# Two attentions share visits to TensorE: riders in one h buffer, turns without beats, and a third engine for the row scaling

## The chip, the cores and the metric

The kernel runs on one core of a Trainium2 chip. The core has TensorE (PE in the profile: matmuls; PEld: its weight loads), VectorE (DVE), ScalarE (ACT), GpSimd (POOL) and a queue of SyncE (SP) that issues the transfers. The metric is the time of one execution on the chip in microseconds, as the median of several runs.

## The reference

A cross attention compresses each batch of 12608 rows to 32 rows h, a second attention lets every row attend to h, and every resulting row goes through a gated layer with a softmax, a normalization and a second weight matrix.

```python
B, N, m, C = (4, 12608, 32, 128)
n_tokens, d_model, d_ff = (50432, 128, 1024)

def mab(q, kv):
    s = scale * (q @ kv.transpose(0, 2, 1))
    s = s - s.max(-1, keepdims=True)
    a = np.exp(s)
    a /= a.sum(-1, keepdims=True) + 1e-09
    return a @ kv
h = mab(I, x)
return mab(x, h).astype(np.float32)
...
h = x @ w_in
h_max = np.max(h, axis=-1, keepdims=True)
e = np.exp(h - h_max)
sm = e / (np.sum(e, axis=-1, keepdims=True) + 1e-09)
solu = h * sm
mu = np.mean(solu, axis=-1, keepdims=True)
var = np.mean((solu - mu) ** 2, axis=-1, keepdims=True)
ln = (solu - mu) / np.sqrt(var + 1e-06) * g_ln
return (ln @ w_out).astype(np.float32)
```

All of it is float32 for the matmuls.

## The kernel before

The rows of a batch are cut into 99 tiles of 128 (the last one shorter), 396 tiles in all. Line numbers here are those of the kernel before.

**The tile's path** (`main` and `soft`). Since h has 32 rows, the second attention's output times `w_in` is the attention's weights times a 32 x 1024 matrix `hs`, made once a batch in `combine`. So a tile's first product is 8 matmuls of 32 rows (line 946) into an h buffer, 128 x 1024 numbers in PSUM. VectorE scales it and takes its minimum (line 984), which frees h. ScalarE takes the exps with their sum (line 994), GpSimd multiplies (line 998), ScalarE squares and sums (line 1009), and VectorE turns blocks of 32 x 32 into `vt` (line 1022). When the four tiles of a group are turned, two streams `products` of 32 steps each follow on TensorE (line 1067), one on row groups 0 and 1 of the array, one on 2 and 3. Their results are evacuated by VectorE or ScalarE (line 1089), and `finish` scales the rows by the normalization, on ScalarE as four instructions (line 1144) or on GpSimd as one (line 1140).

**The attentions.** `p1(b, k)` is the first attention of twelve tiles of batch b: turns of x (line 550), scores (line 654), a small matmul for the common maximum (line 679), exps (line 705), sums (line 736). Batch 0 does this ahead of everything (the `early` branches); for later batches it lies among the tiles of the batch before. `p2(b, j)` is the second attention of up to twelve tiles: scores (line 844), their turning and maximum on VectorE (lines 851 and 853), exps, turns of the weights (line 550), copies (line 885).

**The two h buffers.** Outside the early part, PSUM has two h buffers and two buffers for the streams. A tile's first product, each turn, each score block and each block of sums takes an h buffer and gives it back when its last reader is done. For the scores of `p1` the last reader are the exps.

**Beats.** The first products and the turns use two of TensorE's four row groups. `beats` puts single steps of the stream that uses the other two between them. `turned_rows` turns three blocks to a beat. What uses all rows of the array (scores, sums, the small matmuls) is a visit of its own; the planner charges `SWITCH` = 400 ns for it.

**The order.** A planner (class `Planner`) writes the order of each engine ahead of time: it plays the program through with a cost for each operation, a latency for each crossing between engines (`AFTER`), and priorities (`PR_...`, in tiles). An operation with an alternative (`alt`) goes to the engine that can start it first. Each engine then runs its instructions in that order and waits on semaphores. So a change of a cost or of a priority moves instructions on all engines.

```python
pick = min(
    (o for o in self.ops if o[0].eng == eng and o[1] <= limit),
    key=lambda o: (o[2][1] if o[0].prio is None else o[0].prio, o[3]),
)
```

Of the kernel before, what the change touches and what calls it, by code (L numbers as in the profile page):

```python
# [14 lines left out]
ALU = mybir.AluOpType  # L15
# [5 lines left out]
C = 128  # L21
M = 32
FF = 1024
# [3 lines left out]
PG = 12  # L27
AG = 12
JB = FF // M
JC = 1  # L30
BEAT = 225
EAGER = 120
SWITCH = 400


def cut(total, most, unit):
# [17 lines left out]
TURNS = 3  # L54
HN_MORE = 4
# [3 lines left out]
LATE = -15  # L59
P1_FROM = 5  # L60
P1_GO = -10
P1_STEP = 7.5
P2_AHEAD = 35
P2_START = 24
PR_EX = 1
PR_EV = -20
PR_FI = 20
PR_G2 = 2
PR_HN = -2
PR_MU = 2  # L70
# [3 lines left out]
SLACK = {"PE": 0, "ACT": 100, "DVE": 300, "POOL": 0, "SP": 0}  # L74
# [5 lines left out]
AFTER = {  # L80
    "PE": {"PE": 0, "ACT": 237, "DVE": 236, "POOL": 240, "SP": 290},
    "ACT": {"PE": 245, "ACT": 143, "DVE": 182, "POOL": 101, "SP": 90},
    "DVE": {"PE": 296, "ACT": 168, "DVE": 127, "POOL": 195, "SP": 90},
    "POOL": {"PE": 245, "ACT": 115, "DVE": 114, "POOL": 100, "SP": 90},
    "SP": {"PE": 1076, "ACT": 1040, "DVE": 960, "POOL": 1040, "SP": 1000},
}
# [39 lines left out]
class Planner:  # L126
# [26 lines left out]
    def _step(self, task, value):  # L153
        gen = task[0]
        while True:
# [4 lines left out]
            if isinstance(want, Op):  # L160
                self.seq += 1
                for op in (want, want.alt):
                    if op is None:
                        continue
# [5 lines left out]
                    self.ops.append((op, start, task, self.seq))  # L170
                return
# [75 lines left out]
def set_attention_then_solu_kernel(ctx: ExitStack, tc: tile.TileContext, x, inducing, w_in, w_out, g_ln, out):  # L247
# [66 lines left out]
    EW = Lock()  # L314
# [261 lines left out]
    turned = [Event() for _ in range(NP)]  # L576

    def p1(b, k):
# [35 lines left out]
        for w in () if early else range(2):  # L614
            tr, trel = yield ltr
            d = yield turned_rows(tr, [(xn[:, s, :], P) for s in range(n)], w, RUSH, [d for d, _ in xd], trel)
            closing(d)
# [27 lines left out]
        if not early:  # L645
            (eT, ew), erel = yield lew
        big, rel = yield lpb
        sc = big[:, : PG * M]
        mq = big[:, 512 - C : 512 - C + 4]

        def scores():
# [6 lines left out]
        d = yield Op("PE", (0 if early else SWITCH) + n * 60, scores, ready, rel, ind_ready.after)  # L658
# [66 lines left out]
        d = yield Op("DVE", 435, lambda: nc.vector.transpose(out=ew[:, :n, :].rearrange("p s m -> p (s m)"), in_=eT[:, : n * M]), d)  # L725
        nq = min(4, n)
        rel = None
        if not early:
            give(lpb, big, de)
            big, rel = yield lpb  # L730
        pooled = big[:, 512 - C : 512]

        def gather():
# [6 lines left out]
        dp = yield Op("PE", 74 * n, gather, d, rel)  # L740
        give(lx, xn, dp)
        give(lew, (eT, ew), dp)
# [18 lines left out]
        give(lpb, big, da)  # L761
# [55 lines left out]
    def p2(b, j):  # L817
# [16 lines left out]
        sp, rel = yield bank  # L834
# [17 lines left out]
        give(bank, sp, d)  # L852
# [22 lines left out]
        for w in range(2):  # L875
# [3 lines left out]
            closing(dt)  # L879
# [218 lines left out]
    def finish(b, f):  # L1098
# [34 lines left out]
        for j in js:  # L1133
# [5 lines left out]
            def scaled():  # L1139
                nc.gpsimd.tensor_tensor(out=os[:rows], in0=raw, in1=y[:, i0 : i0 + 4].unsqueeze(2).to_broadcast([rows, 4, C]), op=ALU.mult)  # L1140
# [5 lines left out]
            done = yield Op("ACT", 1170, scaled_act, dy, rel, alt=Op("POOL", 1000, scaled, dy, rel))  # L1146
# [33 lines left out]
    for b in range(NB):  # L1180
        if b:
            for k in range(NP):
                starts.setdefault(NT * (b - 1) + int(P1_FROM + P1_STEP * k), []).append((p1(b, k), PRIO_P1(b, k)))
# [4 lines left out]
    def handover():  # L1188
# [29 lines left out]
        give(EW, ew_b, *done)  # L1218
# [45 lines left out]
```

## Time and profile before

| | |
|---|---|
| median of 3 runs | 1251.52 us (1248.7 to 1261.63) |
| profiled execution | 1254.37 us, span 1252.6 us |
| TensorE, weight loads | busy 96% and 89% of the span |
| VectorE, ScalarE, GpSimd | busy 90%, 90% and 88% |
| DMA | 113.68 MB, mean 91 GB/s |
| matmuls of line 946, of line 1067 | 6336 and 25600 |
| granted TensorE clock, mean | 0.984 |

Each float32 matmul of the program stands in the trace as two, so a step of one stream (two matmuls of the program) is four of the trace, and a double step of both streams, or of one stream and a first product, is eight. Busy time of TensorE is the union of overlapping matmuls. A row of a group names the line, engine, operation, the tiles out<-in, the shapes and the count, then the busy time, the mean length of one in ns, and the idle time of the engine ahead of them with what ended it. The batches overlap only in that the first attention of the next one lies within the tiles of the one before.

### The profile page before, as it was taken

How to read it: one execution, taken by the hardware profiler on the slowest of the kernel's cores; microseconds unless marked ns; L12 is line 12 of the kernel's file. 1: busy time of each engine (PE TensorE's matmuls, PEld its weight loads, DVE VectorE, ACT ScalarE, POOL GpSimd, SP SyncE). 2: the span in 40 equal slices, each digit the busy share in tenths (PEclk: the TensorE clock that was granted, in tenths of full speed). 3: DMA queues.
4: the chain of work that ended last, by engine and by line, in shares of the span. 5: the costliest groups of instructions: out<-in, count | busy, mean ns of one | idle time of the engine just before them, and what ended most of it. 6: DMA issues, size and time to landing. Idle time of an engine off the chain costs nothing. (4 is left out here: it accounts for less than half of the span.)

```text
span 1252.6 us, 78887 instructions
## 1 busy us (share of the span) xinstructions
PE 1200.5 (96%) x35640; PEld 1113.4 (89%) x35640; DVE 1124.9 (90%) x1816; ACT 1127.9 (90%) x2414; POOL 1101.9 (88%) x981
## 2 busy tenths in 40 slices
PE   9889999999999999999999999999999999999995
PEld 7679999999899988999898988889989999988995
DVE  5589999999999998999988987989999999999982
ACT  5479999999899998999878997989989999999994
POOL 2478899899999998999988987987999999999994
PEclk9879999999999999999999999999999999999998
DMA  9562233331224342331223231332121221211111
GB/s 355 179 170 81 80 131 105 114 101 39 86 58 133 106 130 98 81 100 61 80 80 107 64 124 55 110 110 88 57 80 56 61 56 55 55 47 45 22 31 42
DMA packets 118162, 113.68 MB, mean 91 GB/s; under 512 B 76576, under 2 KB 83776, under 8 KB 117696
## 3 DMA queue, kind: packets, MB, share of 16 engines
q1 hardware_dynamic: 117824, 108.62, 28.3%
q8 instruction: 279, 4.57, 1.5%
q14 instruction: 59, 0.48, 0.1%
HBM read 54.30 MB, written 52.18 MB: 85 GB/s over the span
## 5 line engine op out<-in xcount | busy, mean ns | idle before, releaser
L1067 PE MATMUL op<-wc,vt 32*128 32x129 f32 x25600 | 1034.2, 275 | 22.9 <-issue 16.8
L1067 PEld LDWEIGHTS op<-wc,vt 32*128 32x128 f32 x25600 | 989.5, 185 | 62.6 <-issue 48.6
L998 POOL TENSOR_TENSOR eu<-spare,eu 128x1024 f32<-128x1024 f32 x191 | 452.3, 2374 | 33.1 <-ACT eu L994 30.7
L946 PE MATMUL h<-hs,aT 32*128 32x128 f32 x6336 | 436.5, 277 | 4.9 <-DVE spare L984 1.4
L1022 DVE STREAM_TRANSPOSE vt<-eu 128x1024 f32<-128x1024 f32 x330 | 403.9, 1232 | 7.1 <-POOL eu L998 7.1
L946 PEld LDWEIGHTS h<-hs,aT 32*128 32x128 f32 x6336 | 392.2, 189 | 19.1 <-issue 4.4
L1009 ACT ACTIVATE sq<-eu 128x1024 bf16<-128x1024 f32 x330 | 346.7, 1051 | 25.4 <-POOL eu L998 20.9
L998 POOL TENSOR_TENSOR eu<-hn,eu 128x1024 f32<-128x1024 f32 x139 | 329.4, 2373 | 25.3 <-ACT eu L994 24.8
L984 DVE TENSOR_SCALAR_CACHE_REDUCE spare<-h,rn 128x1024 f32<-128x1024 f32 x227 | 285.9, 1263 | 23.3 <-PE h L946 15.8
L984 DVE TENSOR_SCALAR_CACHE_REDUCE hn<-h,rn 128x1024 f32<-128x1024 f32 x169 | 213.1, 1263 | 21.2 <-PE h L946 11.8
L994 ACT ACTIVATE eu<-spare,nm 128x1024 f32<-128x1024 f32 x191 | 217.8, 1141 | 2.9 <-DVE spare L984 2.9
L994 ACT ACTIVATE eu<-hn,nm 128x1024 f32<-128x1024 f32 x139 | 158.5, 1141 | 0.2 <-DVE hn L984 0.2
L1144 ACT ACTIVATE os<-spare,fin 128x128 f32<-128x128 f32 x272 | 85.5, 390 | 5.1 <-DMA out_dram<-os 3.6
L998 POOL TENSOR_TENSOR spare<-spare 128x1024 f32<-128x1024 f32 x36 | 85.5, 2374 | 5.2 <-ACT spare L994 5.1
L1022 DVE STREAM_TRANSPOSE vt<-spare 128x1024 f32<-128x1024 f32 x66 | 81.1, 1229 | 0.9 <-POOL spare L998 0.8
L1009 ACT ACTIVATE sq<-spare 128x1024 bf16<-128x1024 f32 x66 | 69.4, 1052 | 6.9 <-POOL spare L998 6.0
L998 POOL TENSOR_TENSOR spare<-hn,spare 128x1024 f32<-128x1024 f32 x30 | 71.2, 2372 | 2.5 <-ACT spare L994 2.3
L1089 DVE COPY spare<-op 128x258 f32<-128x258 f32 (+1 forms) x113 | 47.0, 420 | 27.4 <-PE op L1067 26.0
L1009 ACT ACTIVATION_READ_ACCUMULATOR sq<-eu 128x1 f32 x330 | 62.8, 190 | 0.0
L1089 ACT COPY spare<-op 128x258 f32<-128x258 f32 (+1 forms) x87 | 31.5, 365 | 23.9 <-PE op L1067 23.5
L550 PE MATMUL h<-ident,xn 32*128 32x32 f32 x1188 | 46.1, 220 | 1.6 <-issue 1.0
L550 PEld LDWEIGHTS h<-ident,xn 32*128 32x128 f32 x1188 | 44.4, 137 | 2.4 <-issue 1.2
(164 smaller groups left out, 1031.4 us busy)
## 6 DMA issues: line engine op xcount, KB each, us to landing
out_dram<-os SPq DMA_DIRECT2D x96, 256.0 KB, 2.6
xT<-xd SPq DMA_DIRECT2D x27, 768.0 KB, 4.9
xn<-in_x_dram SPq DMA_DIRECT2D x21, 768.0 KB, 5.4
xd<-xT SPq DMA_DIRECT2D x21, 768.0 KB, 4.1
dl<-dd SPq DMA_DIRECT2D x396, 1.0 KB, 2.8
xd<-vt SPq DMA_DIRECT2D x7, 768.0 KB, 11.5
spare<-in_x_dram SPq DMA_DIRECT2D x5, 768.0 KB, 12.8
xT<-xd SPq DMA_DIRECT2D x5, 512.0 KB, 4.7
```

Source lines behind the costliest of these rows:

```text
L550: nc.tensor.transpose(out=tr[:h, at : at + M], in_=block[rows, :h], identity=ident[rows, rows])
L946: nc.tensor.matmul(hp[:, cols], lhsT=aT[rows, i // 2, :], rhs=hs[rows, cols], start=True, stop=True)
L984: lambda: nc.vector.tensor_scalar(out=hn, in0=hp, scalar1=rn, scalar2=None, op0=ALU.mult, op1=ALU.min, accum_out=nm),
L994: "ACT", 1133, lambda: nc.scalar.activation(e, hn, AF.Exp, bias=nm, scale=-1.0, accum_out=G["S"][:, s : s + 1]), d, rel, srel,
L998: d = yield Op("POOL", 2330, lambda: nc.gpsimd.tensor_tensor(out=e, in0=hn, in1=e, op=ALU.mult), de, prio=t + PR_MU)
L1009: "ACT", 1040, lambda: nc.scalar.activation(sq, e, AF.Square, scale=1.0 / 32.0, accum_out=G["qe"][:, s, 0:1]), d,
L1022: lambda: nc.vector.transpose(out=G["vtb"][:, : n * FF].rearrange("p (j s t) -> p j s t", j=M, s=n)[:, :, s, :], in_=e.rearrange("p (a f) ...
L1067: nc.tensor.matmul(op[:rows, a - 2 * w, : C + 1], lhsT=vt[q, k, :], rhs=wc[q, k, :], start=(k == 0), stop=(k == JB - 1))
L1089: return lambda: eng(F["raw"][:rows, i0 : i0 + 2, :], op[:rows, :, : C + 1])
L1144: nc.scalar.activation(os[:rows, q, :], raw[:, q, :], AF.Copy, scale=y[:, i0 + q : i0 + q + 1])
```

## The change

**Riders.** The second attention now takes a whole h buffer, with its scores in the upper half. Just before its scores are written into TensorE's order, `visit` looks for scores and sums of the next batch's first attention that are ready or will be ready within `PATIENCE` = 1500 ns of the time at which the visit can start, and puts them into the same visit and into the lower half of the same buffer. A first attention's scores or sums no longer ask for an h buffer themselves: `ride` leaves them with the planner until a visit takes them; when the batch has no visits left, they are a visit of their own. The buffer is given back when all who use it have left. The buffers eT and ew, one lock before, are two.

**Turns in one go.** `turned_rows` issues all its transposes one behind the other, at a cost of 60 + 26 ns a block, with no steps of the other stream between.

**Scaling rows.** VectorE is a third engine that may scale rows, at priority 1000 (so it does only when it has nothing else).

**Numbers.** The streams' own operation takes two beats (`JC`), latencies between engines are 40 ns longer, first attentions start five tiles later, second ones eleven tiles earlier, one buffer goes from hn to eu, and some priorities differ.

```diff
-JC = 1
+JC = 2
...
-TURNS = 3
-HN_MORE = 4
+PATIENCE = 1500
+SCALE_DVE = 1000
+HN_MORE = 3
...
-P1_FROM = 5
+P1_FROM = 10
...
-P2_START = 24
-PR_EX = 1
-PR_EV = -20
+P2_START = 35
+PR_EX = -1
+PR_EV = -60
...
-PR_MU = 2
+PR_MU = -2
...
-SLACK = {"PE": 0, "ACT": 100, "DVE": 300, "POOL": 0, "SP": 0}
+SLACK = {"PE": 0, "ACT": 300, "DVE": 300, "POOL": 0, "SP": 0}
...
-    "PE": {"PE": 0, "ACT": 237, "DVE": 236, "POOL": 240, "SP": 290},
+    "PE": {"PE": 0, "ACT": 277, "DVE": 276, "POOL": 280, "SP": 330},
...
-        def some(i):
-            for k, (block, h) in list(enumerate(blocks))[i * TURNS : (i + 1) * TURNS]:
+        def go():
+            for k, (block, h) in enumerate(blocks):
...
-        count = -(-len(blocks) // TURNS)
-        return Op("PE", count * BEAT, lambda: beats(count, (1 - w,), some), *after, prio=prio)
+        return Op("PE", 60 + 26 * len(blocks), go, *after, prio=prio)
...
+    def ride(b, cost, emit, *after):
+
+        r = dict(cost=cost, emit=emit, after=after, on=Event())
+        if visits[b]:
+            riders[b].append(r)
+            (d,) = yield r["on"]
+        else:
+            big, rel = yield H
+            r["lent"] = dict(big=big, left=1, done=[])
+            d = yield Op("PE", SWITCH + cost, lambda: emit(big), rel, *after)
+        return r["lent"], d
+
+    def visit(b, big, cost, emit, *after):
+        visits[b] -= 1
+        limit = max(when(*after), plan.clock["PE"]) + PATIENCE
+        mine = [r for r in riders[b] if not visits[b] or when(*r["after"]) <= limit]
+        riders[b] = [r for r in riders[b] if r not in mine]
+        lent = dict(big=big, left=1 + len(mine), done=[])
...
+        d = yield Op("PE", SWITCH + cost + sum(r["cost"] for r in mine), go, *after, *(a for r in mine for a in r["after"]))
...
-        d = yield Op("PE", (0 if early else SWITCH) + n * 60, scores, ready, rel, ind_ready.after)
+        if early:
+            d = yield Op("PE", n * 60, lambda: scores(big), ready, rel, ind_ready.after)
+        else:
+            lent, d = yield from ride(b - 1, n * 60, scores, ready, ind_ready.after)
+            sc, mq = lent["big"][:, : PG * M], lent["big"][:, FF - 4 :]
...
-        dp = yield Op("PE", 74 * n, gather, d, rel)
+        if early:
+            dp = yield Op("PE", 74 * n, lambda: gather(big), d)
+        else:
+            lent, dp = yield from ride(b - 1, 50 * n, gather, d)
+            big = lent["big"]
...
-        sp, rel = yield bank
+        big, rel = yield bank
+        sp = big[:, 512:]
...
-        d = yield Op("PE", SWITCH + n * 60, scores, d, rel, hd)
+        lent, d = yield from visit(b, big, n * 60, scores, d, rel, hd)
...
-            done = yield Op("ACT", 1170, scaled_act, dy, rel, alt=Op("POOL", 1000, scaled, dy, rel))
+            on_dve = Op("DVE", 620, scaled(nc.vector.tensor_tensor), dy, rel, prio=SCALE_DVE)
+            done = yield Op("ACT", 1170, scaled_act, dy, rel, alt=Op("POOL", 1000, scaled(nc.gpsimd.tensor_tensor), dy, rel, alt=on_dve))
```

In the orders below a name's last number tells buffers apart; h0 and h1 are the h buffers, op0 and op1 the two streams' results. A row is a line, an operation, out<-in, a shape and a count. Lines 946, 1067, 550, 844, 654, 736 and 1144 of the kernel before are 1005, 1126, 551, 904, 699, 787 and 1203 of the changed one.

TensorE before, a turn of twelve blocks of x in batch 0, behind a tile's first product:

```order
L946 MATMUL h0_663<-hs0_123,aT1_96 128x128 x2
L1067 MATMUL op0_665<-wc_157,vt_65 128x129 x2
L550 MATMUL h1_664<-ident_138,xn0_67 128x32 x6
L1067 MATMUL op1_666<-wc_157,vt_65 128x129 x2
L550 MATMUL h1_664<-ident_138,xn0_67 128x32 x6
```

Each six transposes are followed by a step of the other stream. TensorE in the changed order, a turn of the same buffer:

```order
L1005 MATMUL h1_666<-hs0_123,aT1_96 128x128 x2
L1126 MATMUL op0_667<-wc_157,vt_65 128x129 x2
L551 MATMUL h0_665<-ident_138,xn0_67 128x32 x24
L1126 MATMUL op0_667<-wc_157,vt_65 128x129 x2
L1126 MATMUL op1_668<-wc_157,vt_65 128x129 x2
```

All 24 transposes stand together, and no step stands between them. TensorE in the changed order, a visit of the second attention in batch 0 with two riders (sums of one group from xn and ew, scores of the next one):

```order
L1126 MATMUL op0_667<-wc_157,vt_65 128x129 x2
L1126 MATMUL op1_668<-wc_157,vt_65 128x129 x8
L904 MATMUL h0_665<-xT2_86,h4_0_122 32x384 x4
L787 MATMUL h0_665<-xn0_67,ew_99 32x128 x12
L699 MATMUL h0_665<-xT_85,indT_156 32x384 x4
L1005 MATMUL h1_666<-hs0_123,aT1_96 128x128 x2
```

Before, the three blocks stood apart, each with a buffer of its own; now they follow each other in h0. GpSimd in the order before, at tile 121, where the `finish` of three groups in fin1 scales rows (out os):

```order
L1129 TENSOR_TENSOR fin1_117<-fin1_117 128x12
L1039 TENSOR_SCALAR qe1_105<-st1_106 128x4
L1140 TENSOR_TENSOR os1_101<-spare_66,fin1_117 128x512
L1040 TENSOR_TENSOR qe1_105<-qe1_105 128x4
L998 TENSOR_TENSOR spare_66<-spare_66 128x1024
L998 TENSOR_TENSOR eu_84<-spare_66,eu_84 128x1024
L1140 TENSOR_TENSOR os1_101<-spare_66,fin1_117 128x512
```

Two of the three scalings are GpSimd's, among its multiplies of line 998. ScalarE in the changed order, at tile 123, for the `finish` of the same groups:

```order
L1203 ACTIVATE os1_101<-spare_66,fin1_117 128x128 x4
L1148 COPY spare_66<-op0_667 128x258
L1148 COPY spare_66<-op1_668 128x258
L1203 ACTIVATE os0_100<-spare_66,fin1_117 128x128 x4
L1068 ACTIVATE sq_83,qe1_105<-eu_84 128x1024
L1053 ACTIVATE eu_84,st3_112<-hn2_82,nm3_121 128x1024
L1068 ACTIVATE sq_83,qe2_108<-spare_66 128x1024
L1203 ACTIVATE os1_101<-spare_66,fin1_117 128x128 x4
```

All three scalings are ScalarE's now, with two evacuations of stream results (line 1148) between exps and squares.

Over the whole program ScalarE scales 68 groups of rows before and 80 in the changed order, GpSimd 32 and 14, VectorE none and 6; VectorE evacuates 113 stream results before and 97 after, ScalarE 87 and 103.

More of the change, by code (lines that the diff above doesn't have):

```diff
@@ L80 @@
 AFTER = {
-    "PE": {"PE": 0, "ACT": 237, "DVE": 236, "POOL": 240, "SP": 290},
[L82 to L85, printed above, removed]
+    "PE": {"PE": 0, "ACT": 277, "DVE": 276, "POOL": 280, "SP": 330},
+    "ACT": {"PE": 285, "ACT": 143, "DVE": 222, "POOL": 141, "SP": 130},
+    "DVE": {"PE": 336, "ACT": 208, "DVE": 127, "POOL": 235, "SP": 130},
+    "POOL": {"PE": 285, "ACT": 155, "DVE": 154, "POOL": 100, "SP": 130},
+    "SP": {"PE": 1116, "ACT": 1080, "DVE": 1000, "POOL": 1080, "SP": 1000},
 }
@@ L161, in _step @@
                 self.seq += 1
-                for op in (want, want.alt):
-                    if op is None:
-                        continue
+                op = want
+                while op is not None:
                     start = 0.0
@@ L576, in set_attention_then_solu_kernel, with leave, when, go @@
     turned = [Event() for _ in range(NP)]
+    riders = [[] for _ in range(NB)]
+    visits = [len(g) for g in at_groups]
+    def leave(lent, *done):
+        lent["done"] += done
+        lent["left"] -= 1
+        if not lent["left"]:
+            give(H, lent["big"], *lent["done"])
+    def when(*after):
+        return max([0.0] + [d.end + AFTER[d.eng]["PE"] for a in after for d in (a if isinstance(a, (tuple, list)) else (a,)) if d is not None])
+    def ride(b, cost, emit, *after):
[14 more added lines that the diff above has]
+        lent = dict(big=big, left=1 + len(mine), done=[])
+        def go():
+            emit()
+            for r in mine:
+                r["emit"](big)
+        d = yield Op("PE", SWITCH + cost + sum(r["cost"] for r in mine), go, *after, *(a for r in mine for a in r["after"]))
+        for r in mine:
+            r["lent"] = lent
+            plan.set(r["on"], d)
+        return lent, d
     def p1(b, k):
@@ L724, in p1, with gather @@
             d = yield Op("DVE", 70, lambda: nc.vector.memset(eT[half:, nf * M : n * M], 0.0), d)
-        d = yield Op("DVE", 435, lambda: nc.vector.transpose(out=ew[:, :n, :].rearrange("p s m -> p (s m)"), in_=eT[:, : n * M]), d)
+        wrel = None
+        if not early:
+            leave(lent, de)
+            ew, wrel = yield lew
+        d = yield Op("DVE", 435, lambda: nc.vector.transpose(out=ew[:, :n, :].rearrange("p s m -> p (s m)"), in_=eT[:, : n * M]), d, wrel)
         nq = min(4, n)
-        rel = None
         if not early:
[L729 to L733, printed above, removed]
+            give(ET, eT, d)
+        def gather(big):
+            pooled = big[:, 512 - C : 512]
             for s in range(n):
@@ L760, in p1 @@
         da = yield Op("DVE", 263, add, dp, de, p1_done[b][k - 1].after if k else None)
-        give(lpb, big, da)
+        if early:
+            give(lpb, big, da)
+        else:
+            leave(lent, da)
         dl = yield l_done[b][k]
@@ L1217, in handover @@
             give(OS, o, *done)
-        give(EW, ew_b, *done)
+        give(ET, ew_b[0], *done)
+        give(EW, ew_b[1], *done)
         for a in xn_b:
```

34 lines of the change are left out of this document (18 added, 16 removed).

## The prediction

> **What bounds the kernel now.** I read the page's engine shares first (busy us, share, instructions), then the busy times of five stretches of the program, cut where a batch's first product of line 946 starts. The columns of a stretch are its ends, its length, then the busy time and (x) instruction count of PE, PEld, DVE, ACT and POOL, the granted clock, the DMA share and GB/s.
>
> ```profile
> span 1252.6 us, 78887 instructions
> PE 1200.5 (96%) x35640; PEld 1113.4 (89%) x35640; DVE 1124.9 (90%) x1816; ACT 1127.9 (90%) x2414; POOL 1101.9 (88%) x981
> ```
>
> ```profile
> 96.50:341.70 245.20, 244.26 (x7438) 224.83 (x7437) 235.03 (x392) 233.24 (x501) 222.82 (x191) 1.00 0.30 92
> 341.70:638.00 296.30, 290.57 (x8977) 268.68 (x8970) 280.39 (x451) 276.02 (x581) 277.01 (x251) 1.00 0.31 92
> 638.00:946.90 308.90, 296.79 (x8975) 275.48 (x8977) 277.26 (x450) 280.46 (x599) 269.14 (x233) 0.99 0.29 89
> 946.90:1211.40 264.50, 258.10 (x8186) 249.79 (x8182) 252.52 (x351) 256.63 (x553) 258.98 (x229) 1.00 0.17 45
> 1211.40:1252.60 41.20, 26.95 (x902) 26.22 (x897) 14.39 (x17) 23.12 (x58) 23.65 (x34) 0.88 0.17 46
> ```
>
> No engine stands out. ScalarE (ACT) is busy 233.24/245.20 = 95.1% of what I call batch 0, 276.02/296.30 = 93.2% of batch 1, 280.46/308.90 = 90.8% of batch 2 and 256.63/264.50 = 97.0% of batch 3, which has no next batch to prepare. VectorE (DVE) and GpSimd (POOL) lie within some points of it. TensorE's 96% says little, since its matmuls overlap; I count them instead. When both product streams are ready, 256 of them take 7.63 us, that is 32 double steps of 8 at 0.238 us, or 33.6 a microsecond. At that rate the 7438 matmuls of batch 0 are 90% of what fits, those of batch 1 90%, of batch 2 86%, of batch 3 92%.
>
> ```profile
> 1224.21 7.63 PE L1067 MATMUL op<-wc,vt 32*128 32x129 f32 x256 [0.69 <-DVE vt L1022]
> ```
>
> So TensorE has room of 24, 29 and 42 us in batches 0 to 2, some 95 us in all, partly made of switches and of steps that find only one stream ready. The bound is the interplay of four engines: three of them above 90%, each in a written order, and a late one passes its lateness on. Whole batches, by the matmuls of line 946 (length, PE busy, count, clock, DMA), show how much that costs:
>
> ```profile
> 52.00:341.70 289.70, 113.03 (x1584) 0.96 0.34 101
> 341.70:638.00 296.30, 107.84 (x1584) 1.00 0.31 92
> 638.00:946.90 308.90, 109.44 (x1585) 0.99 0.29 89
> 946.90:1213.00 266.10, 106.17 (x1584) 1.00 0.17 45
> ```
>
> Batches 1 and 2 do what batch 0 does and take 6.6 and 19.2 us longer. The waits (total us, times, longest) name the links:
>
> ```profile
> POOL eu L998 <- ACT eu L994: 55.6, 47, 3.5
> ...
> ACT sq L1009 <- POOL eu L998: 20.9, 31, 2.2
> PE op L1067 <- issue: 16.8, 15, 2.5
> DVE spare L984 <- PE h L946: 15.8, 25, 2.5
> ```
>
> GpSimd waits for ScalarE more than twice as long as the reverse. "issue" is time in which TensorE waited for nothing that the profile shows.
>
> **The change, part by part.** The sum is made against the profiled execution: 1254.4 us, of which 1252.6 are span. That is 2.9 us above the median of 1251.5, so I subtract 2.9 at the end.
>
> *Riders.* In the order of the program 15 of 27 first-attention score blocks and 12 of 27 sums now stand in a visit of the second attention. In the merged visits the riders carry no wait of their own. Before, each was a visit by itself, as the timeline shows (start, length):
>
> ```profile
> 133.70 0.50 PE L1067 MATMUL op<-wc,vt 32*128 32x129 f32 x10
> 134.13 0.85 PE L654 MATMUL h<-xT,indT 128*32 128x384 f32 x8
> 134.91 0.95 PE L1067 MATMUL op<-wc,vt 32*128 32x129 f32 x24
> ...
> 480.96 0.86 PE L736 MATMUL h<-xn,ew 128*32 128x128 f32 x24
> 481.75 0.71 PE L1067 MATMUL op<-wc,vt 32*128 32x129 f32 x14
> ```
>
> The groups give the mean of one such matmul in ns, behind the busy time:
>
> ```profile
> L736 PE MATMUL h<-xn,ew 128*32 128x128 f32 x594 | 22.0, 277 | 0.1
> ...
> L654 PE MATMUL h<-xT,indT 128*32 128x384 f32 x168 | 17.9, 498 | 0.0
> ```
>
> Scores keep products away for 134.91 - 134.13 = 0.78 us. When another block follows at once, they need the 0.85 us less the 0.50 us that the last matmul alone takes, plus one step of 0.05: 0.40. A ride saves 0.38. Sums: 0.79 against 0.86 - 0.28 + 0.03 = 0.61, a saving of 0.18. Together 15 x 0.38 + 12 x 0.18 = 8 us of TensorE; the other bound is the whole visit, 27 x 0.78 = 21 us. I take 8, because the matmuls are still made. The riders also spare a buffer. One score block held one of the two h buffers from its first matmul to the end of its exps, 298.20 to 303.75, 5.6 us:
>
> ```profile
> 298.20 0.57 PE L654 MATMUL h<-xT,indT 128*32 128x224 f32 x8
> ...
> 303.57 0.18 ACT L705 ACTIVATION_READ_ACCUMULATOR eT<-h,small 64x1 f32 x1
> ```
>
> How much of this reaches the end no row tells: at least nothing, at most the 15.8 us in which VectorE waited for h, of which I take little.
>
> *Turns in one go.* Before, a turn stood in beats, with steps of the other stream between; now it stands alone. Durations on both sides:
>
> ```profile
> 484.31 0.32 PE L550 MATMUL h<-ident,xn 32*128 32x32 f32 x6
> ...
> 484.99 0.28 PE L1067 MATMUL op<-wc,vt 32*128 32x129 f32 x2
> ...
> 155.72 0.82 PE L550 MATMUL h<-ident,xn 32*128 32x32 f32 x22
> 156.34 0.38 PE L1067 MATMUL op<-wc,vt 32*128 32x129 f32 x2
> ...
> 333.57 0.51 PE L550 MATMUL h<-ident,a 32*128 32x32 f32 x12
> 333.91 0.58 PE L1067 MATMUL op<-wc,vt 32*128 32x129 f32 x6
> ```
>
> In beats, 24 transposes take 484.31 to 484.99, 0.68 us, and products run beside them. Without products, 22 take 0.62 (so 24 take 0.68) and 12 take 0.34. One go is no shorter; it only loses the steps beside it. The order before has 320 such single steps. They need 160 double steps of 0.238 elsewhere: +38 us of TensorE. The code prices a turn of 12 blocks at 60 + 26 x 12 = 372 ns and one of 6 at 216. By these prices 54 and 74 turns would be 54 x 0.31 + 74 x 0.12 = 26 us shorter than by the rows; I go by the rows.
>
> The Trainium skill, "TensorEngine Tiling (Array Packing)", Performance Considerations, speaks against one go as well: each matmul costs about 60 cycles however few columns it streams, and "Trainium Kernel Development and Optimization", NeuronCore Architecture, gives TensorE 2.4 GHz. By an estimate from these two pages that is 25 ns a transpose and 0.60 us for 24. The trace has 0.68; page and row stand together against the code's 0.37.
>
> TensorE's balance is +38 - 8 = +30 us (bounds +17, with whole visits saved, and +38). It stays hidden as long as the 95 us of room take it.
>
> *Scales and evacuations.* The order moves 12 row scalings to ScalarE and 6 to VectorE, all 18 from GpSimd, and 16 evacuations from VectorE to ScalarE. The groups of these lines:
>
> ```profile
> L1144 ACT ACTIVATE os<-spare,fin 128x128 f32<-128x128 f32 x268 | 84.3, 390 | 5.1 <-DMA out_dram<-os 3.6 <-POOL fin L1129 1.3
> L1089 DVE COPY spare<-op 128x258 f32<-128x258 f32 x108 | 44.9, 419 | 18.0 <-PE op L1067 16.7
> ...
> L1089 ACT COPY spare<-op 128x258 f32<-128x258 f32 x84 | 30.4, 364 | 13.6 <-PE op L1067 13.3
> L1140 POOL TENSOR_TENSOR os<-spare,fin 128x512 f32<-128x512 f32 x29 | 30.2, 1041 | 0.0
> ```
>
> And line 783 by itself, least/median/most ns of one:
>
> ```profile
> L783 DVE TENSOR_SCALAR accn<-acc,small x4: 286/1081/1921, 43.2 to 913.4; 128x128 f32<-128x128 f32 x4
> ```
>
> A scaling on ScalarE is four instructions, 84.3/67 = 1.26 us. ScalarE gets 12 x 1.26 + 16 x 0.36 = +21 us, GpSimd 18 x 1.04 = -19, VectorE -16 x 0.42 = -6.7 and six scalings. No row has a scaling on VectorE; the code's price is 0.62, the nearest rows of an engine are the 1.04 of GpSimd and, for a small VectorE operation on data outside PSUM, line 783's 0.29 to 1.92 us. So +2 to +12, taken 1 us each, +6: VectorE stays as it is. Three of the six stand at the program's very end, where VectorE has nothing else.
>
> Line 783's spread fits a rule in "SBUF — State Buffer", Who interferes with whom, of the Trainium skill: a VectorE operation with two inputs in SBUF and a GpSimd one that reads SBUF lock each other out for a whole instruction. By an estimate from it a scaling could wait for one multiply; line 783 shows such a length, but nothing here shows its cause.
>
> *The rest.* Two product beats to an op, 40 ns more for each crossing between engines, one buffer of hn given to eu, and the priorities change the order and not the work. Nor do the transfers: both orders hold the same DMAs, and in both 21 pairs of large ones (loads of xn and xT, the store of xT) stand directly one behind the other, so I give them nothing either way. The last stretch keeps its 41.2 us, since both orders end with the 64 double steps of the last two groups behind the last transpose. A rider has a wait of another kind: it stays until the next visit comes. In batch 0 five of the nine first-attention groups now have their scores at tile 65 or later, before it was three. Nothing queues behind a waiting rider, since it is not in TensorE's order yet, but the late groups stand closer.
>
> **The sum.** ScalarE ends fullest, so I go by it. By batches (counts of scalings and evacuations of tiles 0 to 98, 99 to 197, 198 to 296 in the two orders) it gets 2 x 1.26 + 3 x 0.36 = 3.6, 11 x 1.26 + 6 x 0.36 = 16.0 and 1.26 - 0.36 = 0.9 us: 789.7 + 20.5 = 810.2 us in the stretches of batches 0 to 2, which last 850.4 us now (92.9% full). Batch 3 gets nothing. Batch 0 shows that 95.1% can be had with the same work, batch 3 that 97.0% is about the most. I take 95.5%, near batch 0: 810.2/0.955 = 848.4, 2 us less than now. 1254.4 - 2.0 - 2.9 = 1249.5, so **1249 us**. What speaks for a fuller ScalarE are the spared buffer holds and switches; what keeps the gain down is that the work moves towards the engine which is waited for already.
>
> **Rivals.** *A, the holes close:* with fewer holds of h, batches 1 and 2 run at batch 0's pace, 6.6 + 19.2 = 25.8 us less: 1226. For it: the excess is waiting, not work. Against it: part of the waiting is TensorE's "issue", whose cause the profile does not show; more work lands on ScalarE. Chance 0.27, range 1212 to 1239. *B, slower, TensorE becomes the bound:* products no longer run beside turns, the order believes in turns of 0.37 us, and in the run of late first-attention groups at a batch's end TensorE falls behind; all of the +30 on the path gives 1281. It decides once 12.5 us, 42% of it, is not hidden. For it: the rows show no gain of one go. Against it: 95 us of room. Chance 0.20, range 1264 to 1281. *C, slower, ScalarE stays at 92.9%:* 810.2/0.929 = 872, +22, 1273. GpSimd then waits even longer for the exps. Chance 0.08. My forecast has 0.45 with a range of its own of 1236 (97.0% full) to 1264.
>
> About 1% (12.5 us) is what a measurement of this kernel can tell from no change. Of the forecast's 0.45, 0.08 lie below 1239. So faster 0.35, same 0.37, slower 0.28. The range from 1224 to 1276 leaves out the ends of A and of B, under 0.2.
>
> **What would show it.** Right: ScalarE's busy time near 1149 us, GpSimd's near 1083, ScalarE 95 to 96% full in batches 0 to 2, turns of 24 at 0.68 us with no product beside them, visits with two riders of about 0.40 + 0.61 + 0.78 = 1.8 us. A is right if batch 2 comes under 295 us. B is right if matmuls a microsecond stay while line 984 waits longer for line 1005's h. The forecast is wrong if the multiplies of GpSimd wait for exps over 80 us in all (C), or if score holds do not fall in number.

## The result, and the profile after

The changed kernel takes 1266.3 us (median of 20 runs, 1257.4 to 1275.0) against 1252.3 (20 runs, 1245.5 to 1261.6): 1.0116 times as long, 95% interval 1.0096 to 1.0135. That is slower by about 1.2%; the forecast was no change. Two executions of kernels below, of 4291 and 5656 us, stand far apart from all others and are left out of the medians.

The profiled execution took 1258.8 us, one of the shorter ones. Its engine shares (busy us, share, instructions), from the page:

```profile
span 1257.0 us, 78975 instructions
PE 1204.4 (96%) x35660; PEld 1125.5 (90%) x35660; DVE 1127.9 (90%) x1803; ACT 1148.5 (91%) x2478; POOL 1086.6 (86%) x966
```

The same five stretches as before, cut at a batch's first product (now line 1005; the first one begins at 96.5 us, inside batch 0): ends, length, busy time and (x) count of PE, PEld, DVE, ACT, POOL, clock, DMA share, GB/s.

```profile
96.50:357.60 261.10, 256.26 (x7736) 239.73 (x7732) 241.98 (x396) 245.68 (x528) 229.63 (x198) 0.99 0.30 92
357.60:659.90 302.30, 293.63 (x8964) 275.18 (x8961) 277.52 (x444) 286.49 (x622) 264.84 (x235) 0.99 0.29 89
659.90:959.10 299.20, 294.55 (x9056) 277.13 (x9053) 279.31 (x451) 286.31 (x614) 267.10 (x237) 1.00 0.30 92
959.10:1217.00 257.90, 250.49 (x8028) 241.70 (x8025) 248.96 (x342) 252.70 (x543) 254.41 (x218) 0.99 0.17 43
1217.00:1257.00 40.00, 26.93 (x846) 25.73 (x838) 17.81 (x20) 22.07 (x54) 21.23 (x34) 0.93 0.17 47
```

Against before, batch 0 loses 261.1 - 245.2 = 15.9 us and batch 1 6.0; batch 2 gains 9.7, batch 3 6.6 and the last stretch 1.2: 4.4 us, the difference of the two spans. The matmuls of batch 0 are now 7736/(33.6 x 261.1) = 88% of what fits, 90% before.

The waits of the whole span (total us, times, longest):

```profile
POOL eu L1057 <- ACT eu L1053: 56.0, 49, 5.1
...
POOL spare L1057 <- ACT spare L1053: 25.4, 19, 4.0
PEld op L1126 <- issue: 24.6, 48, 2.6
DVE hn L1043 <- PE h L1005: 16.3, 24, 3.3
DVE spare L1043 <- PE h L1005: 12.6, 21, 1.7
```

VectorE waits for h as long as before (28.9 us, 27.6 before), GpSimd waits for exps 81 us against 63. No one wait holds the 14 us, so experiments had to find them.

### The profile page after: what moved, and what is told of

Same layout as the page of the kernel before. It is cut to its first block, busy times and chain, and to the rows that moved or that the text cites. A ratio compares the mean times of both kernels' runs of the same rounds, so it can differ in the third digit from the quotient of the medians.

```text
span 1257.0 us, 78975 instructions
## 1 busy us (share of the span) xinstructions
PE 1204.4 (96%) x35660; PEld 1125.5 (90%) x35660; DVE 1127.9 (90%) x1803; ACT 1148.5 (91%) x2478; POOL 1086.6 (86%) x966
## 5 line engine op out<-in xcount | busy, mean ns | idle before, releaser
L1057 POOL TENSOR_TENSOR eu<-spare,eu 128x1024 f32<-128x1024 f32 x140 | 331.5, 2376 | 26.7 <-ACT eu L1053 26.5
L1081 DVE STREAM_TRANSPOSE vt<-eu 128x1024 f32<-128x1024 f32 x282 | 343.9, 1232 | 4.0 <-POOL eu L1057 3.8
L1068 ACT ACTIVATE sq<-eu 128x1024 bf16<-128x1024 f32 x282 | 296.0, 1050 | 6.3 <-POOL eu L1057 3.9
L1053 ACT ACTIVATE eu<-spare,nm 128x1024 f32<-128x1024 f32 x140 | 159.8, 1142 | 2.5 <-DVE spare L1043 2.5
L1057 POOL TENSOR_TENSOR spare<-spare 128x1024 f32<-128x1024 f32 x58 | 137.3, 2372 | 16.2 <-ACT spare L1053 16.1
L1081 DVE STREAM_TRANSPOSE vt<-spare 128x1024 f32<-128x1024 f32 x114 | 139.6, 1232 | 1.4 <-POOL spare L1057 1.2
L1057 POOL TENSOR_TENSOR spare<-hn,spare 128x1024 f32<-128x1024 f32 x56 | 132.5, 2371 | 9.3 <-ACT spare L1053 9.2
L1203 ACT ACTIVATE os<-spare,fin 128x128 f32<-128x128 f32 (+1 forms) x320 | 100.3, 390 | 3.3 <-DVE vt L1081 2.0
L1053 ACT ACTIVATE spare<-spare,nm 128x1024 f32<-128x1024 f32 x58 | 66.2, 1142 | 3.6 <-DVE spare L1043 3.5
L1053 ACT ACTIVATE spare<-hn,nm 128x1024 f32<-128x1024 f32 x56 | 64.0, 1142 | 2.1 <-DVE hn L1043 2.1
```

Source lines behind the costliest of these rows:

```text
L1053: "ACT", 1133, lambda: nc.scalar.activation(e, hn, AF.Exp, bias=nm, scale=-1.0, accum_out=G["S"][:, s : s + 1]), d, rel, srel,
L1057: d = yield Op("POOL", 2330, lambda: nc.gpsimd.tensor_tensor(out=e, in0=hn, in1=e, op=ALU.mult), de, prio=t + PR_MU)
L1068: "ACT", 1040, lambda: nc.scalar.activation(sq, e, AF.Square, scale=1.0 / 32.0, accum_out=G["qe"][:, s, 0:1]), d,
L1081: lambda: nc.vector.transpose(out=G["vtb"][:, : n * FF].rearrange("p (j s t) -> p j s t", j=M, s=n)[:, :, s, :], in_=e.rearrange("p (a f) ...
L1203: nc.scalar.activation(os[:rows, q, :], raw[:, q, :], AF.Copy, scale=y[:, i0 + q : i0 + q + 1])
```

## The experiments

### New orders of the same program; turns in beats again; no riders

Four kernels first. Two ask for nothing new and only make the planner write the order again, one from the kernel before and one from the changed one:

```diff
-BEAT = 225
+BEAT = 226
```

> The kernel before with one planner's price changed by 0.4% (a beat is charged 226 instead of 225 ns). No work changes, only places in the written order. Theory 'turns' (products that no longer run beside turns cost time on TensorE) and theory 'ScalarE' (21 us more work on ScalarE cost time): no change, 1252 within 4 us. Theory 'draw' (each newly written order lands somewhere in a scatter of about 1%, and the change drew a bad one): anything from 1240 to 1266, most likely 5 us or more away from 1252.

> The changed kernel with the same 0.4% on the price of a beat. 'Turns' and 'ScalarE': 1266 within 4 us. 'Draw': 5 us or more away from 1266, to either side, 1252 to 1275.

Measured: the kernel before with 226 ns 1261.1 us (1.0079, 1.0048 to 1.0109), the changed one 1267.1 (1.0126, 1.0096 to 1.0156). The first moved by 9 us, as "draw" has it; the second stayed, where "draw" expected 5 us or more. Later the other neighbour:

> The kernel before with the price of a product beat at 224 ns in place of 225, which asks for nothing new and only makes the planner write the order anew: a second look at the scatter after 226, which came out 1.0079 times as long. 'Draw': 1255 to 1266 us, since the kernel before would be one of the better orders of its family. If the 226 was an accident: 1250 to 1254.

Measured: 1247.0 us (0.9933, 0.9908 to 0.9958), below both ranges that were expected. So 224, 225 and 226 give 1247, 1252 and 1261: a price changed by 0.4%, with the same work, moves the time by 14 us. This scatter of written orders is as large as the result, and no single pair of kernels can be read without it.

The other two take one edit back. Turns in beats again in the changed kernel:

```diff
...
-        return Op("PE", 60 + 26 * len(blocks), go, *after, prio=prio)
+        count = -(-len(blocks) // TURNS)
+        return Op("PE", count * BEAT, lambda: beats(count, (1 - w,), some), *after, prio=prio)
...
```

> The changed kernel with its turns in beats again, three blocks to a beat with steps of the other stream between, at the old price; riders, scaling on VectorE and all numbers as in the changed kernel. 'Turns': TensorE gets back the 38 us worked out, and since 14 us were lost, 1252 or less (1240 to 1254). 'ScalarE': ScalarE keeps its load, 1266 within 5. 'Draw': anything within 1252 to 1275.

And no rider is ever taken along:

```diff
-        if visits[b]:
+        if False:
             riders[b].append(r)
```

> The changed kernel without riders: scores and sums of the first attention always ask for an h buffer and make a visit of their own, all else as in the changed kernel. If riders help as worked out (8 us of TensorE, 27 visits less): 1272 or more. If waiting for a visit and standing close at a batch's end costs more than it saves: 1254 to 1262. 'ScalarE' and 'turns' both say that riders are not the cause: not under 1266.

Measured: 1274.6 us (1.018, 1.015 to 1.0211) with beats and 1258.9 (1.0049, 1.0021 to 1.0077) without riders. Giving the beats back doesn't help. Taking the riders away gains 7 us, which alone would still be within the scatter.

### Numbers against structure

All numbers of before (JC, crossings, starts, slack, priorities) in the changed structure, all new numbers in the structure of before, and only the four start times of before in the changed kernel:

```diff
-LATE = -21
-P1_FROM = 10
-P1_STEP = 7
-P2_START = 35
+LATE = -15
+P1_FROM = 5
+P1_STEP = 7.5
+P2_START = 24
```

> The kernel after (riders, turns in one go, VectorE may scale) with all numbers of the kernel before: one product beat to an op, the old crossings, starts, slack and priorities. 'Numbers' (the loss of 15 to 20 us in batch 0 comes from the new start times, priorities and crossings, and the three edits of structure are worth little): 1250 to 1257 us, batch 0 under 297 us. 'Structure' (riders or turns in one go cost it): 1265 us or more, batch 0 still above 302. 'Draw' (every newly written order lands somewhere in about 1252 to 1270, before standing near the lower end): 1258 to 1275, and the batches that lose are others than in the kernel after.

> The kernel before (visits of their own, turns in beats, no scaling on VectorE) with all numbers of the kernel after. 'Numbers': about 1265 us, with batch 0 above 302 us and batch 3 under 260, as in the kernel after. 'Structure': 1250 to 1257, batch 0 near 290 to 299. 'Draw': 1258 to 1275, with no likeness to the kernel after by batches.

> The kernel after with only the four start times of before (the late start, the two of the first attention's groups, the lead of the second attention's). 'Early' (tiles 0 to 11 take 41.6 us after against 34.4 before because of what is started there): tiles 0 to 11 back under 36 us, batch 0 under 298, in all 1253 to 1260 us. If the starts do not matter: batch 0 stays at 302 to 310 and the time at 1262 to 1270.

Measured: 1277.3 (1.0171, 1.0121 to 1.022), 1250.0 (0.9968, 0.994 to 0.9997) and 1282.4 us (1.0223, 1.0164 to 1.0281). "Numbers" is refuted: with them the old structure is as fast as before. The structure costs 16 us with the new numbers (1266.3 against 1250.0) and over 20 with the old ones. The old start times in the changed kernel gave more than either range that was expected.

### The three edits one by one

With the new numbers, each edit alone and the last pair:

> The kernel before with the numbers of after and with riders alone: turns in beats, no scaling on VectorE. Without riders this kernel took 1250 us. 'Riders cost' (a rider waits for a visit that comes late, first-attention work bunches at tiles 66 to 87, an h buffer is kept until the last of a visit is done with it): 1262 us or more, with tiles 66 to 76 of some batch over 44 us. 'Riders save', as predicted (8 us of TensorE and the holds of h): 1240 to 1248. 'Draw': 1250 +- 8.

> The kernel before with the numbers of after and with turns in one go alone. 'Turns' (products that no longer run beside turns, +38 us of TensorE by the prediction's rows): matmuls a microsecond as high as without, and 1262 us or more if that is on the path; if the room of TensorE takes it, 1250 to 1255. 'Draw': 1250 +- 8.

> The kernel before with the numbers of after and with VectorE as a third choice for row scalings alone; its few scalings cost it about 1 us each, three of them after the last product. 1248 to 1253 us if they are worth nothing; 1260 or more if a scaling in VectorE's order holds up a normalisation that others wait for. 'Draw': 1250 +- 8.

> The kernel after without the scalings on VectorE: riders and turns in one go stay. If the scalings cost the kernel after its time: 1250 to 1256 us. If riders or turns do: 1262 to 1270. With the seven others (none, each alone, each left out, all three) this completes the table of the three edits under one set of numbers: 'draw' expects no edit's mean over four pairs to be above 6 us, 'riders cost' and 'turns' expect a mean of 10 or more for theirs.

Measured, with the kernels already told (us, and times the kernel before):

| riders | one go | VectorE | us | ratio, interval |
|---|---|---|---|---|
| - | - | - | 1250.0 | 0.9968, 0.994 to 0.9997 |
| - | - | yes | 1249.0 | 0.9977, 0.9948 to 1.0006 |
| - | yes | - | 1257.6 | 1.0044, 1.0013 to 1.0075 |
| - | yes | yes | 1258.9 | 1.0049, 1.0021 to 1.0077 |
| yes | - | - | 1269.6 | 1.0141, 1.0076 to 1.0207 |
| yes | - | yes | 1274.6 | 1.018, 1.015 to 1.0211 |
| yes | yes | - | 1267.7 | 1.0123, 1.0071 to 1.0175 |
| yes | yes | yes | 1266.3 | 1.0116, 1.0096 to 1.0135 |

The first row has the buffers of the kernel before; the other rows without riders keep those of the changed kernel (a whole h buffer for the second attention's scores, eT and ew apart), which together with the scalings on VectorE cost nothing (second row).

Mean over the four pairs of ratios: riders +0.0131 (16 us; 0.0173, 0.0203, 0.0079, 0.0067), turns in one go +0.0017 (0.0076 and 0.0072 without riders, -0.0018 and -0.0064 with them), VectorE +0.0012. Riders cost in all four pairs, and more than 10 us on average: "riders cost" stands. Turns in one go have no settled sign; the 8 to 10 us without riders are within what a new order can draw. Why riders cost 20 to 25 us beside turns in beats and 7 to 10 beside turns in one go, as the changed kernel has them, stays open.

### Riders: the wait or the merged visit

What a rider waits for can be read in the trace of the changed kernel. One first-attention group, in the timelines of its engines (start, length):

```profile
460.29 0.80 ACT L650 COPY xT<-h 128x768 f32<-128x768 f32 x1 [0.40 <-PE h L551]
...
477.39 0.85 PE L904 MATMUL h<-xT,h 128*32 128x384 f32 x8
478.06 0.84 PE L787 MATMUL h<-xn,ew 128*32 128x128 f32 x24
478.71 0.83 PE L699 MATMUL h<-xT,indT 128*32 128x384 f32 x8
479.47 0.38 PE L1005 MATMUL h<-hs,aT 32*128 32x128 f32 x2
...
485.50 0.54 DVE L778 STREAM_TRANSPOSE ew<-eT 128x384 f32<-128x384 f32 x1
...
524.49 0.64 PE L904 MATMUL h<-xT,h 128*32 128x256 f32 x8
524.94 0.84 PE L787 MATMUL h<-xn,ew 128*32 128x128 f32 x24
525.60 0.83 PE L699 MATMUL h<-xT,indT 128*32 128x384 f32 x8
```

Its xT is complete at 461.1, its scores ride at 478.7: 17.6 us. Its weights are ready at 486.0, its sums ride at 524.9: 38.9 us, until the next visit of the second attention (line 904), 47.1 us behind the one before. One kernel with the new numbers and riders alone lets riders wait like this, but then gives each a visit and a buffer of its own:

```diff
         if visits[b]:
             riders[b].append(r)
-            (d,) = yield r["on"]
-        else:
-            big, rel = yield H
-            r["lent"] = dict(big=big, left=1, done=[])
-            d = yield Op("PE", SWITCH + cost, lambda: emit(big), rel, *after)
+            yield r["on"]
+        big, rel = yield H
+        r["lent"] = dict(big=big, left=1, done=[])
+        d = yield Op("PE", SWITCH + cost, lambda: emit(big), rel, *after)
...
```

> The kernel with the numbers of after and riders alone (1269.6 us; without riders 1250.0), but here a rider only waits until a visit has been made and then stands by itself, with its own switch and its own h buffer. 'Waiting': the loss comes from the wait for the visit, which pushes scores and sums to tiles 63 and later; then this kernel loses it too, 1265 us or more, and if the merged visits save the 8 us that the prediction gave them, about 1278. 'Merged': the loss comes from the long visits and from the h buffer that is kept until the last of a visit is done; then it is back at 1248 to 1255 us.

In the same kernel with riders alone, another lets only the scores ride:

```diff
-            lent, dp = yield from ride(b - 1, 50 * n, gather, d)
-            big = lent["big"]
+            big, rel = yield H
+            lent = dict(big=big, left=1, done=[])
+            dp = yield Op("PE", SWITCH + 50 * n, lambda: gather(big), d, rel)
```

> The kernel with the numbers of after and riders alone (1269.6 us; without riders 1250.0), but only the scores ride; the sums stand by themselves as soon as they are ready. If the second wait of each group does the harm (sums that are ready 20 to 30 us before the next visit, and keep a buffer of x and one of the weights so long): 1248 to 1257 us. If the scores' wait does it: 1262 or more.

Measured: 1283.5 us (1.0221, 1.0165 to 1.0278) with the wait alone, 1267.9 (1.0106, 1.0005 to 1.0206) with riding scores alone. The waits of all 27 groups, summed from the traces (last copy of xT to the first matmul of the scores, and turned weights to the sums), the score blocks at tile 63 or later of 99 in batches 0 to 2, and how long tiles 63 to 88 take (first product to first product) in the three batches together:

| kernel (all but the first with the new numbers) | to scores, us | to sums, us | late | tiles 63 to 88, us | median, us |
|---|---|---|---|---|---|
| before | 112 | 99 | 3, 3, 3 | 235 | 1252.3 |
| without edits | 108 | 94 | 3, 4, 3 | 243 | 1250.0 |
| one go, VectorE | 147 | 104 | 4, 3, 4 | 248 | 1258.9 |
| scores ride | 289 | 73 | 5, 5, 5 | 262 | 1267.9 |
| riders alone | 301 | 351 | 5, 5, 5 | 281 | 1269.6 |
| wait alone | 347 | 292 | 5, 6, 5 | 277 | 1283.5 |
| after | 302 | 339 | 5, 5, 5 | 265 | 1266.3 |

The wait costs 1283.5 - 1250.0 = 33 us; merging gives 1283.5 - 1269.6 = 14 back, no more than the scatter. The scores' wait alone does harm too: without the sums' wait the kernel is nearly as slow, within its wide interval, but tiles 63 to 88 take 19 us more than without edits, and 38 more with both waits, so how the harm is shared stays open. What the wait does in time: with riders alone, the groups 2 to 6 of batch 0 have their scores 3 to 9 tiles later (29, 43, 51, 63 and 66 against 26, 34, 43, 55 and 60), and five of nine then stand at tile 63 or later, where a batch's visits end and a rider becomes a visit of its own. Tiles 63 to 88 of batch 0 without the edits and with riders alone, busy times by stretch:

```profile
236.80:312.10 75.30, 74.25 (x2302) 69.17 (x2299) 71.64 (x121) 72.43 (x156) 67.75 (x59) 1.00 0.27 81
```

```profile
238.00:334.90 96.90, 95.60 (x2872) 87.70 (x2868) 83.75 (x148) 86.72 (x187) 80.36 (x73) 1.00 0.29 90
```

More work lies in the stretch (ScalarE 86.7 us against 72.4), and it is done less tightly: ScalarE is busy 89% of the time and VectorE 86%, against 96 and 95%. The waits of these two stretches, without and with riders:

```profile
POOL eu L998 <- ACT eu L994: 1.8, 3, 0.8
...
DVE spare L984 <- PE h L946: 0.6, 2, 0.5
```

```profile
POOL eu L1061 <- ACT eu L1057: 10.8, 7, 3.7
DVE hn L1047 <- PE h L1009: 4.4, 3, 2.9
```

Half of it comes back in the last tiles of a batch, nothing in the first ones: with riders and without, tiles 88 to 99 of the three batches take 79.9 and 98.8 us, tiles 0 to 63 557.3 and 557.6. That the mixture of many groups at once is what spoils the tightness is an inference from these rows; no run changed the crowding without the wait.

### Is TensorE's time on the path?

Three kernels. In two the order of every engine is unchanged (new numbers, no edits) and TensorE gets more to do: each transpose of a turn twice, or the first products of one tile in five twice.

```diff
+                    for _ in range(2):
-                    nc.tensor.transpose(out=tr[:h, at : at + M], in_=block[rows, :h], identity=ident[rows, rows])
+                        nc.tensor.transpose(out=tr[:h, at : at + M], in_=block[rows, :h], identity=ident[rows, rows])
```

> The kernel before with the numbers of after (1250.0 us), the same order of instructions on every engine, with each transpose of a turn made twice: 1988 more at 0.028 us, up to +56 us of TensorE, less what runs beside the products of the other stream. 'Room' (TensorE's spare time hides it, as the prediction took for +30): 1250 to 1256 us. 'TensorE on the path': 1275 or more. In between, the time added for each us of TensorE prices the turns in one go by themselves.

```diff
-                        nc.tensor.matmul(hp[:, cols], lhsT=aT[rows, i // 2, :], rhs=hs[rows, cols], start=True, stop=True)
+                        for _ in range(2 if t % 5 == 2 else 1):
+                            nc.tensor.matmul(hp[:, cols], lhsT=aT[rows, i // 2, :], rhs=hs[rows, cols], start=True, stop=True)
```

> The kernel before with the numbers of after (1250.0 us), the same order on every engine, with the products into h made twice for one tile in five: 79 x 16 = 1264 more matmul records, 38 us at 33.6 a microsecond. The doubled turns added 47.7 us, but they also made the copies of ScalarE wait longer for a turn. 'TensorE on the path': what counts is TensorE's time, wherever it is added; 1276 us or more (0.7 and more of each us). 'Turn latency': products do not hold up copies of turns, so TensorE's room hides them: 1250 to 1260.

In the third, turns in one go are priced as the rows have them:

```diff
-        return Op("PE", 60 + 26 * len(blocks), go, *after, prio=prio)
+        return Op("PE", 57 * len(blocks), go, *after, prio=prio)
```

> The kernel with the numbers of after and turns in one go alone (1257.6 us; in beats 1250.0), with the turn of 12 blocks priced at 684 ns, as the rows of the trace have it, in place of 372. 'Price': the loss of 8 us came from an order that believed in short turns: back to 1247 to 1253. 'TensorE' (the steps beside a turn are lost whatever its price) or 'draw': 1255 to 1265.

Measured: 1297.7 us (1.0357, 1.0302 to 1.0411) for doubled transposes, 1303.8 (1.0441, 1.036 to 1.0521) for doubled products, 1259.6 (1.0075, 1.0046 to 1.0104) for the price. The price explains nothing: 1257.6 with the wrong one.

But added TensorE time lands on the end: +47.7 and +53.8 us. The traces show how much was added, and it is more than the 56 and 38 us that were expected. The turns, each from its first transpose to its last, add up to 53.7 us without doubling and 121.3 with it: 68 us more. The products of a tile take 0.79 us and doubled 1.78: 79 x 0.99 = 78 us more, since the second matmuls find no steps of a stream beside them (30 matmuls start within the 0.79 us, 49 within the 1.78). So in both kernels some 0.7 of the added time lands on the end. No run added time to another engine in the same way; that TensorE's time counts more than theirs isn't shown.

The waits for turns (last row) do grow with doubled transposes. The whole span without any doubling, and that link with doubled transposes:

```profile
DVE hn L984 <- PE h L946: 19.6, 23, 3.6
DVE spare L984 <- PE h L946: 14.6, 27, 1.4
...
ACT xT L606 <- PE h L550: 6.0, 6, 3.2
```

```profile
ACT xT L607 <- PE h L551: 28.0, 34, 2.5
```

With doubled products this link stays small and VectorE waits for h instead:

```profile
DVE spare L985 <- PE h L947: 29.1, 38, 2.7
DVE hn L985 <- PE h L947: 27.9, 33, 3.2
...
ACT xT L606 <- PE h L550: 12.2, 15, 1.5
```

57.0 us against 19.6 + 14.6 = 34.2 without the doubling. "Turn latency" alone is refuted: in both places the added time counts.

### Do small gains add up?

> The kernel before with the numbers of after and a product beat priced at 224 ns: the two changes that each came out below the kernel before (1250.0 and 1247.0 us), together. If such gains add up: 1240 to 1246 us. If they are two draws from one scatter: anywhere from 1245 to 1262.

Measured: 1260.0 us (1.0083, 1.0046 to 1.0119). Two changes that each came out below the kernel before give a slower kernel together: two draws. The fastest kernel found remains the one before with a beat at 224 ns, 1247.0 us. This is also a second draw of the kernel without edits, and measured from its 1260.0 us riders alone cost 10 us and the wait alone 24.

One thing holds in spite of the scatter, over all kernels without doubled work. The nine in which riders ride or wait take 1.0106 to 1.0223 times the kernel before; the nine in which none does, the kernel before among them, take 0.9933 to 1.0083 times. Tiles 63 to 88 of the three batches take 262 to 286 us in the first nine and 235 to 250 in the others.

## Why the prediction was wrong, step by step

**Busy times.** Right: ScalarE 1148.5 us (1149 predicted), GpSimd 1086.6 (1083), VectorE 1127.9 (unchanged from 1124.9). The scalings on VectorE, taken at 1 us each:

```profile
L1199 DVE TENSOR_TENSOR os<-spare,fin x6: 683/1026/2703, 911.6 to 1250.7; 128x512 f32<-128x512 f32 x5, 96x512 f32<-96x512 f32 x1
```

The edit is worth nothing either way, as costed. The rule that was cited from the Trainium skill ("SBUF — State Buffer", Who interferes with whom) let a scaling wait for one GpSimd multiply. This trace agrees. The longest of the six, with GpSimd beside it:

```profile
1222.71 2.70 DVE L1199 TENSOR_TENSOR os<-spare,fin 128x512 f32<-128x512 f32 x1
...
1222.50 2.36 POOL L1057 TENSOR_TENSOR eu<-spare,eu 128x1024 f32<-128x1024 f32 x1
```

It ends 0.55 us after the multiply (1225.41 and 1224.86). The three scalings that start during a multiply, 1.36, 1.50 and 2.70 us long, all end 0.55 us after its end; the three with no multiply beside them take 0.68 to 0.69 us.

**The sum by ScalarE's fill.** ScalarE was busy 245.7 + 286.5 + 286.3 = 818.5 us of the 862.6 of batches 0 to 2, 94.9% (95.5 taken). The fill was nearly right, and yet the stretches are 14.2 us longer than the 848.4 forecast: 8.7 for work that ScalarE does here rather than before or after these stretches (818.5/0.955 = 857.1), 5.5 for the fill. The median lies another 7.5 us above this execution. The fill was taken near batch 0 of before, and that was a lucky batch: 289.5 us from its first product to that of the next, but 294.7 and 298.8 at 224 and 226 ns.

**The failed step** is in "The rest": "A rider has a wait of another kind: it stays until the next visit comes", five groups instead of three at tile 65 or later, "the late groups stand closer", and all of it costed at nothing because nothing queues behind a waiting rider. The position was right: batch 0 has five at tiles 64, 66, 72, 80 and 86. The cost was not: the wait alone measured 33 us (24 by the other draw of the kernel without edits), and in the changed kernel the riders with all they save cost 7 to 10 us; without them it took 1258.9. Nothing has to queue on TensorE for it. The groups that wait come late and fall together with others in tiles 63 to 88, and there the time is lost; that the crowding is how the wait costs is the inference named above. Rival B named the late groups, but only as the place where the turns' +30 would land; no rival gave the wait a cost of its own.

**Riders' saving.** A merged visit of two riders takes 1.84 to 2.08 us from its first matmul to the next one behind it (1.8 predicted). From the last matmul ahead of it that is 2.04 to 2.28 us, against 0.98 + 0.98 + 0.99 for the three alone where only the wait was kept; 12 x 0.67 + 3 x 0.33 = 9 us of TensorE, 8 predicted. The mechanism was right, the size in part by luck: scores save 0.33 and not 0.38 us, sums 0.34 and not 0.18. In the time of the kernel merging brings 14, too near the scatter to tell from 9.

**Turns.** The term of +38 us was too large. The prediction let nothing run beside a turn in one go. The trace of turns in one go alone shows products that start before the turn's end, in 109 of its 129 turns:

```profile
347.77 0.85 PE L1126 MATMUL op<-wc,vt 32*128 32x129 f32 x24
348.44 0.45 PE L551 MATMUL h<-ident,a 32*128 32x32 f32 x10
348.67 0.38 PE L1126 MATMUL op<-wc,vt 32*128 32x129 f32 x2
348.71 0.23 PE L551 MATMUL h<-ident,a 32*128 32x32 f32 x2
```

Counted in the traces (matmuls missing against 33.6 a microsecond around turns, less what is missing just before them), the turns cost TensorE 37 us in beats and 54 in one go: +17, and +12 to +18 when the stretch counted around a turn is made shorter or longer. The end measured +8 to +10 us without riders and -2 to -8 with them.

**Room of 95 us.** Wrong. TensorE's missing matmuls are little of a reserve: some 0.7 of the time added to it in an unchanged order came out at the end. So B was right that TensorE's time is on the path and wrong about what would put it there. Its sign, the longer wait of line 1043 for h, is absent (28.9 against 27.6 us).

**A and C.** Batch 2 came to 299 us, above the 295 of A. C's sign appeared (GpSimd waits for exps 81 us, above 80), but not its cause, since ScalarE was 94.9% full.

**The batch start.** A part that no step had: tiles 0 to 11 (first product to first product) take 41.6 us after, 34.4 before. All seven kernels with turns in one go and the new priorities take 39 to 42 (the four old start times don't help), the twelve others that were read take 33 to 36. One tile further the gap is smaller, 43.4 us against 38.9. In the changed kernel:

```profile
90.84 0.87 PE L1126 MATMUL op<-wc,vt 32*128 32x129 f32 x12 [2.43 <-issue]
91.64 1.51 PE L904 MATMUL h<-xT,h 128*32 128x384 f32 x8
...
93.29 0.58 DVE L911 STREAM_TRANSPOSE s<-h 128x384 f32<-128x384 f32 x1 [3.05 <-PE h L904]
...
97.60 1.15 ACT L1053 ACTIVATE eu<-hn,nm 128x1024 f32<-128x1024 f32 x1 [6.21 <-DVE hn L1043]
```

The fifth visit of the second attention stands at 91.6 us. VectorE waits 3.05 us for its scores ahead of the next normalisations, and ScalarE 6.21 us for those. In six of the seven this visit comes at 90 to 92 us, in the others at 95 or later; but with the four old start times it comes at 102 and the start is as long, so it isn't the whole cause.

The first row adds a piece. TensorE stood idle for 2.43 us with nothing named that it waited for. The trace also holds the packets of 16 KB by which its instructions arrive, one in 4.0 us at the median: the one that landed at 89.4 us had come 9.5 us behind the one before it, and TensorE went on 1.4 us after the landing. All seven kernels with the long start have such a pause of 1.0 to 2.8 us between 89 and 99 us, of the thirteen others only the one with doubled transposes. Between 75 and 1210 us such pauses (over 1 us long, ending within 1.8 us of the landing of a packet that came more than 5.5 us behind the last) add up to 14.0 us before, 0 at 224 ns, 9.5 after, 9.7 with riders alone, 6.8 without edits, 18.3 with the wait alone and 23.3 with riding scores. Part of the scatter, and part of what the last two kernels lost, may lie there; no run changed the arrival of the packets, so that stays open.

## What to carry to other kernels

Work that is held back until it can share a visit saves the switch and pays with the distance to the next visit; price that distance for everything that follows it (here the same work, crowded into later tiles), even if nothing stands behind it in the queue. Where an engine runs at 90% of its own best rate, test whether the rest is room by doing a part of its work twice in an unchanged order, and read from the trace how much time that added. And where a planner writes the order, change a number that means nothing first: its scatter (14 us here) is what any single comparison has to beat.

## What was not expected of the hardware

Some 0.7 of the time added to TensorE came out at the end (47.7 us of 68 for 1988 added transposes, 53.8 of 78 for added products) in a kernel in which four engines are each busy 88 to 96% and none stands out by the page. And a turn of 12 transposes doesn't block TensorE for its whole length: the next products began 0.23 us after its first transpose (348.44 to 348.67), while its last two were still to come. A row scaling on VectorE that began during a GpSimd multiply ended 0.55 us after it, three times of three.
